# A recurrent attention loop that streams a quarter of its weights: other blocks streamed, other blocks held in PSUM, and a fixed slot for every load

## The chip, the cores and the metric

The kernel runs on one core of a Trainium2 chip. The metric is the time of one execution on the device in microseconds (us). The kernel before takes 2891.25 us, the median of 8 runs (2883.82 to 2897.93). The engines are named as the profile names them: PE (TensorE) multiplies, PEld is its weight load, DVE (VectorE) and ACT (ScalarE) do elementwise work, POOL (GpSimd) copies and issues some DMAs, SP (SyncE) issues most DMAs. Every engine works through its own queue in program order; semaphores make it wait for another engine or a DMA.

## The reference

Two independent results are laid side by side in the output: `a` from a recurrent attention, `b` from a long convolution (a state-space layer).

```python
def _A_ref(x, mem0, Wq, Wk, Wv, Wo, seg_len):        # x 1*2048*1024, 32 heads of 128, seg_len 32
    mem = mem0                                        # 8 rows of 1024
    for s in range(n_seg):                            # 64 segments
        h = concat([mem, x[segment s]], axis=1)       # 40 rows
        q, k, v = h @ Wq, h @ Wk, h @ Wv              # each 1024 -> 32*128
        p = softmax(mask(q @ k.T * scale))            # 40*40 a head
        o = (p @ v) @ Wo                              # 32*128 -> 1024
        mem = o[:, :8]                                # the next segment needs it
        outs.append(o[:, 8:])
```

So segment s+1 can't begin its projections before segment s has multiplied by the last block of `Wo`. Each of the four weights is 1024 x 4096 in bf16, 8 MB; together they are larger than the SBUF that the loop leaves free.

## The kernel before

**Order of the whole.** Part B (the convolution, `part_b`) runs first, and beside it the kernel projects those rows of `x` that need no recurrence (8 of each 32), stores them in DRAM (`PKd`), and copies the weight blocks that will be streamed into DRAM tiles of their own (`WD`, `streamed_copies`). Then comes part A's loop of 64 steps (L289 to L479), one step a segment, with only the 32 rows that need the recurrence in `hT`. A last stage multiplies the rows set aside (`OLd`) by `Wo`.

**Weight blocks.** The weights are cut into 64 blocks of 128 x 2048 in bf16 (512 KB). A block of k, q or v is named (matrix, half t, kc): eight blocks kc = 0..7 make one accumulation of 128 x 512 in `quads` (L293). Below, `k04` stands for ("k", 0, 4). A block of `Wo` is ("o", u), here `o5`; 16 of them are used in `oproj` (L393). In a step PE uses the blocks in this order: k0 (8), q0 (8), k1 (8), q1 (8), v0 (8), v1 (8), o (16). Transposes (`tr`), scores, and the products with the probabilities (`pv`) stand between. A k, q or v block is four matmuls of 128x512, an o block eight of 128x256.

**Three homes of a block.** 46 blocks stay in SBUF through the loop (`RESIDENT`, in the profile `W_k`, `W_q`, `W_v`, `W_o`). 16 blocks are loaded from DRAM in every step; the list is `STREAM` and `STREAM_O`. Two blocks, `KEPT`, stay in PSUM (two banks each) and are copied to SBUF by DVE when they are wanted: `fetch` (L261) makes two copies of 128x512 words by `words` (L251, in the trace L252). Streamed and fetched blocks both lie in the pool `wst`, which has four places of 512 KB, here called slots.

**Who sets the order.** The order of part A is written out by hand (`manual_schedule`). `unit` (L224) is called where PE's matmuls of a block are written; for a streamed block it takes the next slot and issues the load on SP (L230). SP runs ahead of PE as far as slots are free: a load is issued when the block that held its slot before has been used by PE, and the loads leave SP in the order in which the blocks are used. Before the change the pool is one ring of four: the 18 streamed and fetched blocks of a step take the slots in turn, in the order of their `unit` and `fetch` calls, so a fetched block also takes its turn in the ring. `fetch(("q", 0, 0))` stands behind the k0 accumulation (L407), `fetch(("o", 8))` behind the first half of the output projection (L461). DVE makes each copy where it stands in its own queue: q00's just behind the copy of the new memory rows into `hT` (L476, end of the step before), o8's just behind the probabilities of the second half (L459).

**The end of a step.** After o15, DVE copies the result (L470), PE transposes the memory rows (L475), DVE copies them to `hT` (L476), and k00 of the next step begins. POOL issues the loads of the next step's `xt` and `pk` and the writes of `OLd` and of the output (L273, L278, L477, L479).

The functions that the diff touches:

Of the kernel before, what the change touches and what calls it, by code (L numbers as in the profile page):

```python
# [10 lines left out]
BF16 = mybir.dt.bfloat16  # L11
F32 = mybir.dt.float32
# [8 lines left out]
HALF_PI = float(np.pi / 2.0)  # L21


STREAM = {("k", 0): (0, 4), ("q", 0): (0, 4), ("k", 1): (0, 4), ("q", 1): (0, 4), ("v", 0): (0, 4), ("v", 1): (0, 4)}
STREAM_O = (0, 3, 5, 8, 11, 13)

KEPT = {("q", 0, 0): 2, ("o", 8): 2}


def weight_blocks(Wq, Wk, Wv, Wo):  # L30
# [13 lines left out]


def streamed_keys():
    return [key for key in [(m, t, kc) for (m, t), kcs in STREAM.items() for kc in kcs] + [("o", u) for u in STREAM_O] if KEPT.get(key) != 2]


def streamed_copies(ctx, tc, src):  # L50
    nc = tc.nc
    dram = ctx.enter_context(tc.tile_pool(name="a_wd", bufs=1, space=bass.MemoryType.DRAM))
    out, copies = {}, []
    for key in streamed_keys():
        part = KEPT.get(key, 0)
        t_ = dram.tile([128, 2048 - 1024 * part], BF16, name="WD_%s" % "_".join(str(i) for i in key))
        copies.append(lambda t_=t_, key=key, part=part: nc.sync.dma_start(
            out=t_[:].rearrange("e (h d) -> e h d", d=1024) if key[0] == "o" else t_[:], in_=src(key)[:, part:] if key[0] == "o" else src(key)))
        out[key] = t_
    return out, copies  # L60

# [99 lines left out]

RESIDENT = [(m, t, kc) for t in range(2) for m in "kq" for kc in range(8)] + [("v", t, kc) for t in range(2) for kc in range(8)] + [("o", u) for u in range(16)]
RESIDENT = [key for key in RESIDENT if key not in streamed_keys() and key not in KEPT]


# [13 lines left out]
def part_a(ctx, tc, x, mem0, src, WD, HE, seg_len, out_a, ahead, W_res, rest):  # L179
    nc = tc.nc  # L180
# [14 lines left out]

    ctx.enter_context(tc.manual_schedule())
    ctx_w = rest.ctx
    wst = ctx_w.enter_context(tc.tile_pool(name="a_wst", bufs=4, side="right"))
    wres = ctx_w.enter_context(tc.tile_pool(name="a_wres", bufs=1, side="right"))
    for key in rest:  # L200
        load_resident(tc, wres, src, key, W_res)
# [19 lines left out]
    nc.gpsimd.affine_select(out=BDL[:], in_=BDL[:], compare_op=ALU.is_ge, fill=0.0, base=0, pattern=[[-8, 4], [-32, 4]], channel_multiplier=1)  # L221
    nc.gpsimd.affine_select(out=BDL[:], in_=BDL[:], compare_op=ALU.is_ge, fill=0.0, base=7, pattern=[[8, 4], [32, 4]], channel_multiplier=-1)

    def unit(key):  # L224
        if key in W_res:
            return W_res[key]
        if key in kept:
            return ahead_of.pop(key)
        t_ = wst.tile([128, 2048], BF16, name="wst", tag="w")
        nc.sync.dma_start(out=t_[:], in_=WD[key][:])  # L230
        return t_

# [15 lines left out]
    ps_k = ctx_l.enter_context(tc.tile_pool(name="a_keep", bufs=1, space=PSUM))  # L248
    kept, ahead_of = {}, {}

    def words(out, in_):  # L251
        nc.vector.tensor_scalar(out=out.bitcast(I32), in0=in_.bitcast(I32), scalar1=0, scalar2=None, op0=ALU.bitwise_or)  # L252

    for key, n_ in KEPT.items():
        t_ = wst.tile([128, 2048], BF16, name="wst", tag="w")
        nc.sync.dma_start(out=t_[:].rearrange("e (h d) -> e h d", h=2) if key[0] == "o" else t_[:], in_=src(key))
        kept[key] = [ps_k.tile([128, 512], F32, name="keep", tag="keep%d" % (len(kept) * 2 + n)) for n in range(n_)]
        for n in range(n_):
            words(kept[key][n][:], t_[:, 1024 * n:1024 * n + 1024])

    def fetch(key):  # L261

        t_ = wst.tile([128, 2048], BF16, name="wst", tag="w")
        for n in range(2):
            if n < KEPT[key]:
                words(t_[:, 1024 * n:1024 * n + 1024], kept[key][n][:])
            else:
                nc.sync.dma_start(out=t_[:, 1024:2048], in_=WD[key][:])
        ahead_of[key] = t_

    def load_pk(j):
        pk = pers.tile([128, 768], BF16, name="pk", tag="pk")
        nc.gpsimd.dma_start(out=pk[:], in_=PKd[j])  # L273
        return pk

    def load_xt(j):
        xt = work.tile([128, KC, XM], BF16, name="xt", tag="F")
        nc.gpsimd.dma_start(out=xt[:].rearrange("p k r -> p (k r)"), in_=XTd[j])  # L278
        return xt

    def put_xt(xt):
        nc.gpsimd.tensor_copy(out=hT[:, :, 0:XM], in_=xt[:])
# [3 lines left out]

    put_xt(load_xt(0))
    pk = load_pk(0)
    for s in range(NS):  # L289
        vl = pk[:, 512:768].rearrange("p (t e) -> p t e", t=2)  # L290
        kl, ql = ([pk[:, 256 * t + o:256 * t + o + 128].rearrange("p (a g k) -> p a g k", a=4, g=4) for t in range(2)] for o in (0, 128))

        def quads(m, t, kcs, a=None):  # L293
            if a is None:

                a = (ps_sc if (m, t) == ("q", 0) else ps_acc).tile([128, 512], F32, name="acc", tag="sc" if (m, t) == ("q", 0) else "acc")
            for kc in kcs:
                w = unit((m, t, kc))
                for g in range(4):
                    nc.tensor.matmul(a[32 * g:32 * g + 32, :], lhsT=hT[:, kc, :], rhs=w[:, 512 * g:512 * g + 512],  # L300
                                     start=(kc == 0), stop=(kc == KC - 1), tile_position=(0, 32 * g), skip_group_check=True)
            return a

        def evac(a, tag):
            q = work.tile([128, 512], BF16, name="ev", tag=tag)
            nc.scalar.copy(out=q[:], in_=a[:])  # L306
            return q
# [70 lines left out]
        def pv_x(t, V, pb, lbs):  # L378

            p = (ps_pv, ps_sc)[t].tile([128, 4, 128], F32, name="pv", tag=("pv", "sc")[t])  # L380
            pv(p[:], t, V, pb, lbs)
            return p
# [10 lines left out]
        def oproj(po, us, oT):  # L393
            for u in us:
                w = unit(("o", u))
                for hh in range(2):
                    h = 2 * u + hh
                    for qt in range(4):
                        nc.tensor.matmul(po[32 * qt:32 * qt + 32, :], lhsT=oT[:, h % 4, (h % 16) // 4, :],  # L399
                                         rhs=w[:, 1024 * hh + 256 * qt:1024 * hh + 256 * qt + 256],  # L400
                                         start=False, stop=(h == 31), tile_position=(0, 32 * qt), skip_group_check=True)
# [2 lines left out]


        a = quads("k", 0, range(KC))
        fetch(("q", 0, 0))  # L407
        k0 = evac(a, "A")
        KT0 = new_kt(0)
        a = quads("q", 0, range(KC))  # L410
# [47 lines left out]
        spread_l(lb1[:], S1[1][:, 0, :], 0, 16, SL)  # L458
        L1 = left_blocks(S1)  # L459
        oproj(pp[:, 1, :], range(0, 8), o0)  # L460
        fetch(("o", 8))  # L461
        pv1 = pv_x(1, V1, pk[:, 0:512].rearrange("p (a b) -> p a b", a=4), [lb1[:].rearrange("p a k -> p (a k)")])
        o1 = evac_o(pv1, "B")
        pv_l(pl_, 1, V1, L1)
# [7 lines left out]
        if s + 1 < NS:  # L472
            pt_o = ps_pv.tile([128, 2, 4, SL], BF16, name="tro", tag="pv")
            for j in range(2):
                nc.tensor.transpose(out=pt_o[:, j, :, :].rearrange("p a b -> p (a b)"), in_=osb[:, 128 * j:128 * j + 128], identity=ident[:])  # L475
            nc.vector.tensor_copy(out=hT[:, :, XM:SL].rearrange("p (q j) r -> p j q r", j=2), in_=pt_o[:, :, :, XM:SL])  # L476
        nc.gpsimd.dma_start(out=OLd[s], in_=ob[:, 1, :])  # L477

        nc.gpsimd.dma_start(out=out_a[s * SL:s * SL + SL, :].rearrange("r (q d) -> q r d", q=4), in_=osb)  # L479
# [3 lines left out]
    with tc.tile_pool(name="a_eo", bufs=1) as eo, tc.tile_pool(name="a_ew", bufs=16) as ew, \  # L483
# [3 lines left out]
        for u in range(16):  # L487
            if u in (0, 2, 4, 6):
# [3 lines left out]
                for n in range(2):  # L492
                    (nc.vector.tensor_copy if n == 0 else nc.scalar.copy)(
                        out=ol[b][:, 16 * n:16 * n + 16, :, :], in_=raw[:, :, 16 * n:16 * n + 16, :].rearrange("p s h k -> p h s k"))
            w = ew.tile([128, 2048], BF16, name="we", tag="we")
# [3 lines left out]
        for u in range(16):  # L499
            for hh in range(2):  # L500
                h = 2 * u + hh
# [594 lines left out]
def kernel(  # L1096
# [25 lines left out]
    src = weight_blocks(A_Wq.rearrange("d h e -> d (h e)"), A_Wk.rearrange("d h e -> d (h e)"),  # L1122
                        A_Wv.rearrange("d h e -> d (h e)"), A_Wo.rearrange("h e d -> (h e) d"))
    WD, copies = streamed_copies(ctx, tc, src)
    ahead = Ahead(ctx, tc, A_x[0], src, seg_len)
    ctx_w = ctx.enter_context(ExitStack())
# [12 lines left out]
    with ExitStack() as ctx_a:  # L1139
        part_a(ctx_a, tc, A_x[0], A_mem0[0], src, WD, A_Wo.shape[0] * A_Wo.shape[1], seg_len, out_a, ahead, W_res, rest)  # L1140
# [35 lines left out]
```

## Time and profile before

| what | value |
|---|---|
| median of 8 runs | 2891.25 us (2883.82 to 2897.93) |
| the profiled execution's own time | 2889.88 us |
| its span in the profile | 2888.2 us |
| mean granted TensorE clock | 0.917 of full |
| PE, DVE, ACT, POOL busy over the span | 72%, 52%, 34%, 18% |
| one step of the loop, mean of steps 5 to 60, from k00 to k00 | 27.77 us |
| streamed loads | 1024 of 512 KB, 16 a step |

The profile's page gives, by part: busy time of each engine, the span in 40 slices, the DMA queues, the chain of work that ended last, the costliest groups of instructions, and the DMA issues. In a group's line the name left of the arrow is written and those to the right are read: `acc<-wst,hT` is a matmul with a streamed or fetched block, `acc<-W_k,hT` one with a block that stays. `[0.85 <-DMA wst<-WD_k]` at the end of a timeline line is the engine's idle time before it and what ended it. The loop lies in slices 13 to 39 of 40.

### The profile page before, as it was taken

How to read it: one execution, taken by the hardware profiler on the slowest of the kernel's cores; microseconds unless marked ns; L12 is line 12 of the kernel's file. 1: busy time of each engine (PE TensorE's matmuls, PEld its weight loads, DVE VectorE, ACT ScalarE, POOL GpSimd, SP SyncE). 2: the span in 40 equal slices, each digit the busy share in tenths (PEclk: the TensorE clock that was granted, in tenths of full speed). 3: DMA queues.
4: the chain of work that ended last, by engine and by line, in shares of the span. 5: the costliest groups of instructions: out<-in, count | busy, mean ns of one | idle time of the engine just before them, and what ended most of it. 6: DMA issues, size and time to landing. Idle time of an engine off the chain costs nothing.

```text
span 2888.2 us, 76070 instructions
## 1 busy us (share of the span) xinstructions
PE 2077.2 (72%) x32791; PEld 1126.1 (39%) x32838; DVE 1515.5 (52%) x2882; ACT 970.9 (34%) x1394; POOL 516.1 (18%) x801
## 2 busy tenths in 40 slices
PE   1478777846797477777777777777777777777747
PEld 0246444532342144444444344444444444443423
DVE  7577676766984144544544445454454444544430
ACT  4767787741121122222222222222222222222210
POOL 2254434541001111111111111111111111111100
PEclk8699898978898699999999999999999999999978
DMA  4546654525336899999998998999999899998991
GB/s 112 150 147 168 177 158 123 149 86 159 104 117 227 313 323 326 325 325 315 315 328 312 315 324 310 322 314 321 308 326 320 309 323 312 326 316 304 319 308 43
DMA packets 354722, 734.94 MB, mean 254 GB/s; under 512 B 111606, under 2 KB 179190, under 8 KB 352336
## 3 DMA queue, kind: packets, MB, share of 16 engines
q1 hardware_dynamic: 316770, 655.39, 67.4%
q0 software_dynamic: 21840, 52.65, 5.6%
q10 hardware_dynamic: 15774, 22.03, 2.3%
q8 instruction: 257, 4.21, 0.6%
q14 instruction: 81, 0.66, 0.1%
HBM read 675.04 MB, written 67.37 MB: 257 GB/s over the span
## 4 chain that ended last, share of the span: by engine, by line
DMA 40%; PE 23%; issue 18%; ACT 7%; DVE 7%; POOL 4%; SPq 0%; ACTq 0%; POOLq 0%; DVEq 0%
DMA wst<-WD_k 14%; PE acc L300 12%; DMA wst<-WD_o 12%; DMA wst<-WD_v 6%; DMA wst<-WD_q 4%; PE pp L399 3%; ACT ev L306 2%; PE pe L505 2%; DMA olr<-OLd 1%; ACT sn L888 1%; ACT oT L386 1%; PE pro L128 1%; POOL us L772 1%; POOL us L773 1%; PE ups L767 1%
## 5 line engine op out<-in xcount | busy, mean ns | idle before, releaser
L300 PEld LDWEIGHTS <-hT 128*32 128x32 bf16 x12288 | 328.5, 98 | 540.9 <-issue 249.3
L300 PE MATMUL acc<-wst,hT 128*32 128x512 bf16 x3072 | 317.6, 399 | 242.9 <-DMA wst<-WD_k 100.6
L306 ACT CAST ev<-acc 128x512 bf16<-128x512 f32 x384 | 225.1, 586 | 482.7 <-PE acc L300 482.1
L399 PEld LDWEIGHTS <-oT 128*32 128x32 bf16 x8192 | 218.8, 100 | 251.7 <-issue 171.4
L399 PE MATMUL pp<-wst,oT 128*32 128x256 bf16 x3072 | 162.8, 287 | 173.0 <-DMA wst<-WD_o 136.6
L312 DVE COPY KT<-tr 128x512 bf16<-128x512 bf16 x128 | 54.3, 424 | 358.9 <-PE tr L311 358.9
L300 PE MATMUL acc<-W_k,hT 128*32 128x512 bf16 x3072 | 230.9, 406 | 0.0
L300 PE MATMUL acc<-W_q,hT 128*32 128x512 bf16 x3072 | 221.1, 390 | 0.0
L399 PE MATMUL pp<-W_o,oT 128*32 128x256 bf16 x5120 | 221.0, 284 | 0.0
L300 PE MATMUL acc<-W_v,hT 128*32 128x512 bf16 x3072 | 211.4, 379 | 0.0
L338 DVE TENSOR_REDUCE mx<-sc 128x8 f32<-128x320 f32 x128 | 62.2, 486 | 236.4 <-PE sc L331 236.4
L252 DVE TENSOR_SCALAR wst<-keep 128x512 int32<-128x512 int32 x256 | 164.2, 683 | 5.9 <-DMA wst<-WD_k 0.9
L386 ACT CAST oT<-pv 128x512 bf16<-128x512 f32 x128 | 75.3, 588 | 245.2 <-PE pv L372 239.1
L470 DVE CAST ob<-pp 128x256 bf16<-128x256 f32 x64 | 27.2, 425 | 239.5 <-issue 236.3
L312 ACT COPY QT<-tr 128x512 bf16<-128x512 bf16 x128 | 75.0, 586 | 213.5 <-PE tr L311 204.4
L1062 PE MATMUL yp<-Bt,mi 128*128 128x512 bf16 x379 | 116.1, 412 | 32.9 <-DVE Bt L1016 15.0
L980 PE MATMUL hps<-KT,MF 128*128 128x512 bf16 x374 | 100.6, 414 | 50.0 <-DVE x L991 26.4
L319 POOL COPY KT<-pk 128x128 bf16<-128x128 bf16 x128 | 38.2, 299 | 528.8 <-PE sc L331 519.3
L278 POOL DMA_DIRECT2D xt<-XTd x64 | 36.2, 565 | 503.5 <-PE pp L372 245.0
L128 PE MATMUL pro<-xTl,wsl 128*128 128x512 bf16 x492 | 115.4, 384 | 8.8 <-DVE ua L769 4.6
L864 DVE SCALAR_TENSOR_TENSOR nr<-kM,ptt 128x656 f32<-128x656 f32 x128 | 106.0, 828 | 20.7 <-ACT kM L863 17.4
L340 ACT ACTIVATE sc<-sc 128x320 f32<-128x320 f32 x128 | 54.0, 422 | 186.7 <-DVE sc L339 165.2
(266 smaller groups left out, 3838.5 us busy)
## 6 DMA issues: line engine op xcount, KB each, us to landing
wst<-WD_o SPq DMA_DIRECT2D x320, 512.0 KB
wst<-WD_k SPq DMA_DIRECT2D x256, 512.0 KB, 5.1
wst<-WD_v SPq DMA_DIRECT2D x256, 512.0 KB, 5.3
wst<-WD_q SPq DMA_DIRECT2D x192, 512.0 KB
Ud<-ux POOLq DMA_DIRECT2D x16, 1024.0 KB, 5.0
uq<-Ud SPq DMA_DIRECT2D x32, 512.0 KB, 4.9
pk<-PKd POOLq DMA_DIRECT2D x64, 192.0 KB, 5.1
wsl<-in_A_Wk_dram SPq DMA_DIRECT2D x16, 512.0 KB
```

Of the source, the lines that this page charges most:

```text
L128: nc.tensor.matmul(a[:], lhsT=w[:, kc, 128 * j:128 * j + 128], rhs=xTl[:, kc, :, :].rearrange("p s k -> p (s k)"), start=(kc == 0), stop=( ...
L252: nc.vector.tensor_scalar(out=out.bitcast(I32), in0=in_.bitcast(I32), scalar1=0, scalar2=None, op0=ALU.bitwise_or)
L300: nc.tensor.matmul(a[32 * g:32 * g + 32, :], lhsT=hT[:, kc, :], rhs=w[:, 512 * g:512 * g + 512], start=(kc == 0), stop=(kc == KC - 1), til ...
L306: nc.scalar.copy(out=q[:], in_=a[:])
L312: eng(out=dst, in_=p[:, i, :, :, :])
L338: nc.vector.tensor_reduce(out=mx[:], in_=sc, axis=AX.X, op=ALU.max)
L386: nc.scalar.copy(out=o[:], in_=p[:].rearrange("p a (g q) -> p a g q", g=4))
L399: nc.tensor.matmul(po[32 * qt:32 * qt + 32, :], lhsT=oT[:, h % 4, (h % 16) // 4, :], rhs=w[:, 1024 * hh + 256 * qt:1024 * hh + 256 * qt + ...
L505: nc.tensor.matmul(pe[b][n][:], lhsT=ol[b][:, hi, :, :].rearrange("p s k -> p (s k)"), rhs=wos[u][:, 1024 * hh + 512 * n:1024 * hh + 512 * ...
L864: v.scalar_tensor_tensor(out=nrs[e // 4][:, e % 4].rearrange("p f t j -> p f (t j)"), in0=kM[:], scalar=MAGIC, in1=ptv, op0=ALU.subtract, ...
L980: pe.matmul(ps[:], lhsT=MF[:, 4 * rr + mc, cs, 128 * kc:128 * kc + 128], rhs=rhs, start=(i == 0 and mc == 0), stop=(i == 1 and mc == 3))
L1062: pe.matmul(yp[:], lhsT=m_[:, cs, kc, :], rhs=Bt[:, kc, half, j, c_, :], start=(n == 0), stop=(n == 15))
```

## The change

The number of streamed blocks (16), of kept blocks (2), of slots (4) and the computation stay the same. What is different:

- which blocks are streamed: of k0 and q0 before 0, 4 and 4 (with q00 kept), after k00, k06 and q03 (with k04 and q05 kept); of `Wo` before 0, 3, 5, 11, 13 (with o8 kept), after 0, 4, 8, 11, 14;
- the slots: each load takes slot number (count of loads) mod 4, so in every step k00, k14, v04, o4 take slot 0; k06, q10, v10, o8 slot 1; q03, q14, v14, o11 slot 2; k10, v00, o0, o14 slot 3;
- a kept block takes the slot of the block named beside it in `KEPT`: k04 that of o14, between o14's use and k10's load; q05 that of k06, between k06's use and q10's load;
- `fetch(("k", 0, 4))` stands at the end of a step, behind the copy into `hT`; `fetch(("q", 0, 5))` stands where q00's stood in the code, behind k0; there is no fetch in the output projection any more.

```diff
-STREAM = {("k", 0): (0, 4), ("q", 0): (0, 4), ("k", 1): (0, 4), ("q", 1): (0, 4), ("v", 0): (0, 4), ("v", 1): (0, 4)}
-STREAM_O = (0, 3, 5, 8, 11, 13)
-
-KEPT = {("q", 0, 0): 2, ("o", 8): 2}
+
+STREAM = {("k", 0): (0, 6), ("q", 0): (3,), ("k", 1): (0, 4), ("q", 1): (0, 4), ("v", 0): (0, 4), ("v", 1): (0, 4)}
+STREAM_O = (0, 4, 8, 11, 14)
+
+KEPT = {("k", 0, 4): ("o", 14), ("q", 0, 5): ("k", 0, 6)}
+SLOTS = 4
...
-    wst = ctx_w.enter_context(tc.tile_pool(name="a_wst", bufs=4, side="right"))
+    wst = ctx_w.enter_context(tc.tile_pool(name="a_wst", bufs=1, side="right"))
...
+    place, loads = {}, [0]
+
     def unit(key):
         if key in W_res:
             return W_res[key]
         if key in kept:
             return ahead_of.pop(key)
-        t_ = wst.tile([128, 2048], BF16, name="wst", tag="w")
+        place[key] = loads[0] % SLOTS
+        loads[0] += 1
+        t_ = wst.tile([128, 2048], BF16, name="wst", tag="w%d" % place[key])
         nc.sync.dma_start(out=t_[:], in_=WD[key][:])
         return t_
...
     def fetch(key):
 
-        t_ = wst.tile([128, 2048], BF16, name="wst", tag="w")
+        t_ = wst.tile([128, 2048], BF16, name="wst", tag="w%d" % place.get(KEPT[key], SLOTS - 1))
         for n in range(2):
-            if n < KEPT[key]:
-                words(t_[:, 1024 * n:1024 * n + 1024], kept[key][n][:])
-            else:
-                nc.sync.dma_start(out=t_[:, 1024:2048], in_=WD[key][:])
+            words(t_[:, 1024 * n:1024 * n + 1024], kept[key][n][:])
         ahead_of[key] = t_
...
     put_xt(load_xt(0))
     pk = load_pk(0)
+    fetch(("k", 0, 4))
     for s in range(NS):
...
         a = quads("k", 0, range(KC))
-        fetch(("q", 0, 0))
+        fetch(("q", 0, 5))
         k0 = evac(a, "A")
...
         oproj(pp[:, 1, :], range(0, 8), o0)
-        fetch(("o", 8))
...
             nc.vector.tensor_copy(out=hT[:, :, XM:SL].rearrange("p (q j) r -> p j q r", j=2), in_=pt_o[:, :, :, XM:SL])
+            fetch(("k", 0, 4))
```

The rest of the diff drops the case of a block kept in part, and gives the loads that fill PSUM before the loop slots 0 and 1.

More of the change, by code (lines that the diff above doesn't have):

```diff
@@ L46, in streamed_keys @@
 def streamed_keys():
-    return [key for key in [(m, t, kc) for (m, t), kcs in STREAM.items() for kc in kcs] + [("o", u) for u in STREAM_O] if KEPT.get(key) != 2]
+    return [key for key in [(m, t, kc) for (m, t), kcs in STREAM.items() for kc in kcs] + [("o", u) for u in STREAM_O]]
 def streamed_copies(ctx, tc, src):
@@ L54, in streamed_copies @@
     for key in streamed_keys():
[L55 to L58, printed above, removed]
+        t_ = dram.tile([128, 2048], BF16, name="WD_%s" % "_".join(str(i) for i in key))
+        copies.append(lambda t_=t_, key=key: nc.sync.dma_start(
+            out=t_[:].rearrange("e (h d) -> e h d", h=2) if key[0] == "o" else t_[:], in_=src(key)))
         out[key] = t_
@@ L252, in words @@
         nc.vector.tensor_scalar(out=out.bitcast(I32), in0=in_.bitcast(I32), scalar1=0, scalar2=None, op0=ALU.bitwise_or)
-    for key, n_ in KEPT.items():
-        t_ = wst.tile([128, 2048], BF16, name="wst", tag="w")
+    for i, key in enumerate(KEPT):
+        t_ = wst.tile([128, 2048], BF16, name="wst", tag="w%d" % i)
         nc.sync.dma_start(out=t_[:].rearrange("e (h d) -> e h d", h=2) if key[0] == "o" else t_[:], in_=src(key))
-        kept[key] = [ps_k.tile([128, 512], F32, name="keep", tag="keep%d" % (len(kept) * 2 + n)) for n in range(n_)]
-        for n in range(n_):
+        kept[key] = [ps_k.tile([128, 512], F32, name="keep", tag="keep%d" % (2 * i + n)) for n in range(2)]
+        for n in range(2):
             words(kept[key][n][:], t_[:, 1024 * n:1024 * n + 1024])
     def fetch(key):
-        t_ = wst.tile([128, 2048], BF16, name="wst", tag="w")
+        t_ = wst.tile([128, 2048], BF16, name="wst", tag="w%d" % place.get(KEPT[key], SLOTS - 1))
         for n in range(2):
-            if n < KEPT[key]:
-                words(t_[:, 1024 * n:1024 * n + 1024], kept[key][n][:])
-            else:
-                nc.sync.dma_start(out=t_[:, 1024:2048], in_=WD[key][:])
+            words(t_[:, 1024 * n:1024 * n + 1024], kept[key][n][:])
         ahead_of[key] = t_
```

## The prediction

> **What bounds the kernel now.** I read the page's slices and chain first, to see which stage and which resource end the time:
>
> ```profile
> span 2888.2 us, 76070 instructions
> ...
> DMA  4546654525336899999998998999999899998991
> GB/s 112 150 147 168 177 158 123 149 86 159 104 117 227 313 323 326 325 325 315 315 328 312 315 324 310 322 314 321 308 326 320 309 323 312 326 316 304 319 308 43
> ...
> DMA 40%; PE 23%; issue 18%; ACT 7%; DVE 7%; POOL 4%; SPq 0%; ACTq 0%; POOLq 0%; DVEq 0%
> DMA wst<-WD_k 14%; PE acc L300 12%; DMA wst<-WD_o 12%; DMA wst<-WD_v 6%; DMA wst<-WD_q 4%; PE pp L399 3%; ACT ev L306 2%; PE pe L505 2%; DMA olr<-OLd 1%; ACT sn L888 1%; ACT oT L386 1%; PE pro L128 1%; POOL us L772 1%; POOL us L773 1%; PE ups L767 1%
> ```
>
> The loop is slices 13 to 39; there the largest links of the chain are the streamed loads. About 320 GB/s looks like a full DMA, but single microseconds of the loop reach 422 GB/s, so the loads are not at a ceiling of bytes. I then asked for the waits in 1200 to 2800 us, and for the tile wst:
>
> ```profile
> PE pp L399 <- DMA wst<-WD_o: 120.6, 163, 2.1
> PE acc L300 <- DMA wst<-WD_k: 90.8, 101, 2.5
> PE acc L300 <- DMA wst<-WD_v: 24.1, 31, 1.7
> PE acc L300 <- DMA wst<-WD_q: 14.4, 34, 1.2
> ```
>
> ```profile
> L252 DVE TENSOR_SCALAR wst<-keep x226: 677/680/693, 1219.8 to 2777.5; 128x512 int32<-128x512 int32 x113
> ...
> DMA to landing us min/median/max: 3.9/5.2/6.9
> ```
>
> PE loses 250 us in 57 steps, 4.4 us a step, to loads, and a load needs 5.2 us from issue to landing. The timeline of one step shows the slots:
>
> ```profile
> 2004.04 1.29 DVE L252 TENSOR_SCALAR wst<-keep 128x512 int32<-128x512 int32 x2
> 2004.06 0.40 PE L300 MATMUL acc<-wst,hT 128*32 128x512 bf16 x4 [0.33 <-PE tro L475]
> ...
> 2004.50 1.49 SPq L230 DMA_DIRECT2D wst<-WD_k  x2
> ...
> 2009.21 0.40 PE L300 MATMUL acc<-wst,hT 128*32 128x512 bf16 x4 [0.85 <-DMA wst<-WD_k]
> ...
> 2020.84 0.40 PE L300 MATMUL acc<-wst,hT 128*32 128x512 bf16 x4
> ...
> 2024.60 1.27 DVE L252 TENSOR_SCALAR wst<-keep 128x512 int32<-128x512 int32 x2
> ...
> 2026.21 0.40 PE L399 MATMUL pp<-wst,oT 128*32 128x256 bf16 x8 [0.52 <-ACT oT L386]
> ...
> 2031.37 1.29 DVE L252 TENSOR_SCALAR wst<-keep 128x512 int32<-128x512 int32 x2
> 2031.39 0.40 PE L300 MATMUL acc<-wst,hT 128*32 128x512 bf16 x4 [0.33 <-PE tro L475]
> ```
>
> k00 is used at 2004.06, and SP issues k10 into its slot at 2004.50; PE uses k10 at 2009.21 after a stall. v14 is used at 2020.84; its slot goes to o8, which DVE brings only at 2024.60 and PE uses at 2026.21: for 5.4 us no load could use that slot.
>
> Over steps 5 to 60 I paired each load's issue with its landing and its first matmul in the trace. Means, time 0 being k00's first matmul:
>
> | load | issue | takes | used | waits in slot |
> |---|---|---|---|---|
> | k04 | -3.78 | 5.36 | 1.68 | 0.11 |
> | k10 | 0.45 | 5.04 | 5.75 | 0.26 |
> | k14 | 2.16 | 5.16 | 7.47 | 0.14 |
> | v00 | 6.20 | 5.59 | 12.33 | 0.55 |
> | o0 | 12.78 | 5.43 | 18.53 | 0.33 |
> | o13 | 20.15 | 5.13 | 25.57 | 0.29 |
>
> With two loads still in flight at the issue one takes 5.06 us, with three 5.57: the loop is bound by slot time, not bytes. The budget of a step: 4 slots x 27.77 = 111.1 us = 16 loads x 5.27 (84.4) + landing to end of use (13.1) + slots taken by the kept blocks + 1.3 (rest). The kept part: q00 from o11's end (24.82) to its own (27.77 + 3.15) is 6.1 us, o8 from 17.78 to 23.94 is 6.2, together 12.3.
>
> **The change part by part.**
>
> *Copies by DVE.* Still two fetches of 2 x 0.68 us a step. o8's leaves the output projection, where 8 waits on it cost PE 5.3 us in all: 0.1 us a step. k04's stands where q00's copy stands now: it starts with the step (2004.04 against 2004.06) and takes 1.29, so k04 can start at 1.31. Without that wait PE would be there at 0.87 (the shortest k00 to k04 in the trace): 0.44 us of new wait. Today k04 comes at 1.68, so this is no loss against today. q05's copy waits for k06's last matmul: 1.31 + 2 x 0.215 + 0.41 = 2.15, and the copy ends at 3.5. PE would be at q05 at about 3.2, so PE waits some 0.3. Behind that copy DVE next has the copy to KT (L312), at 2008.40 (4.3) in the step shown: covered; without that cover it would delay the scores by as much. The added fetch before the loop is at most 1.3 us, once.
>
> *Kept slot time.* k04: o14's end to k04's end. o13's end to k00 is 1.76; o14 is one block (0.2) later, so 1.55 + 1.31 + 0.41 = 3.3. q05: from 2.15 to 3.55 + 0.41, 1.8. Together 5.1 instead of 12.3: 7.2 us of slot time a step set free.
>
> *The fixed slots.* That saving isn't even. Slots 0 and 2 hold no kept block, slot 1 holds q05, slot 3 holds k04 and then must bring k10. SP can issue k10 only after k04's use: 1.31 + 0.41 + 0.05 = 1.77 instead of 0.45. k14 and all later loads stand behind it in SP's queue; k14 goes out at 2.10 (one issue is 0.32), which is no later than today's 2.16, and q10 at about 4.0, q14 at 4.3 (today 4.20). Follow slot 3 with today's durations: k10 1.77 + 5.04, used at 6.85, end 7.26; v00 issued 7.3, takes 5.59, used 12.95, end 13.35; o0 13.4 + 5.43, used 18.9, end 19.3; o14 19.35 + 5.2 (the median), used 24.6, end 25.0; to the next k00 another 1.55. A step of 26.6 us, if PE is never late for these four. Today it is late: v00 and o0 wait 0.55 and 0.33 in their slots, and the least wait is 0.04 to 0.05, so 0.8 us. Sum: 27.4 us.
>
> The same sum for today's ring checks the method. Each slot there passes nine blocks in two steps; one slot has k10, v00, o0, o11, q00, q10, v10, o5, k00: 42.0 (its eight loads) + 8 x 0.46 + 6.1 = 51.8 in two steps, 25.9 a step, the other pair of slots 26.4, against 27.77 found. So waits add 1.4 to 1.9 there, and 0.8 in mine is the low end; I take 0.8 because k10 and o14 are to be waited for by PE itself, as k14 and k04 are now (0.14, 0.11).
>
> *Bounds of what no row shows.* The latency of k10 when issued beside the writes of OLd and the output, into an emptier queue: from 4.7 (loads whose predecessor had 1.5 to 2.5 us to go) to 5.4 (k04's today, beside the load of pk). I take 5.04, k10's own row. If all four loads took 5.57 (three in flight), slot 3 needs +1.0 us; waits in the slots as large as the ring's (1.9) add 1.1; no waits at all, -0.8.
>
> *Other queues.* No POOL or ACT instruction moves; the 16 loads keep their size and order of issue. The rest of the program is unchanged apart from which blocks are loaded once.
>
> *Sum.* 27.4 instead of 27.77 is -0.35 us, rounded to -0.3 for the k06 to q05 wait that may leak into slot 3; x 63 = -19 us. The profiled execution took 2889.88 (span 2888.2), so 2871; it stands 1.4 below the median, which gives 2872.
>
> The Trainium skill, page "DMA: Bandwidth & Descriptors", section on the anatomy of one DMA, gives about 2.0 us plus bytes over 436 GB/s for a software-issued transfer; as an estimate 512 KB would take 3.2 us. The trace's minimum is 3.9 and its median 5.2, so I don't use it. By it a slot would turn over in 3.7 us, neither kernel would wait for slots, and the change would bring nothing.
>
> **The rivals.**
>
> *A, all freed slot time comes through.* (111.1 - 7.2) / 4 = 25.97 us a step, -1.8 x 63 = -113: 2778. If the fuller queue takes half of the way from 5.27 to 5.57 a load, +0.6 us: about 2815. For it: the budget closes to 1%. Against: slot 3's own round of 26.6 us before any wait, and PE waits in order, so one slow slot holds the other three.
>
> *B, slower: slot 3's round becomes the bound at a fuller queue's latency.* Place: k10, v00, o0 and o14, seen first at the first matmul of k1, 1.1 us later than today (6.85 against 5.75). My four durations have a mean of 5.32; the step is 27.77 again when the mean is 5.41, and that is where it decides. With three loads in flight at all four issues (5.57) the step is 26.6 + 0.8 + 1.0 = 28.4: +0.65 x 63 = +41, 2931. For it: loads that spread evenly keep the queue full, and today's loads in the full stretch take 5.4 to 6.1. Against: k10 is issued with one load or two in flight, and o8's stop in the ring is gone, where o5 to o8 holds 1.66 us at the least, in which o8 can land.
>
> *C, no change.* Slot 3's round replaces the ring's at the same length (26.6 + 1.1): 2880 to 2900.
>
> **How the numbers follow.** This forecast 0.35 (2855 to 2882), A 0.13, B 0.32, C 0.20. What a measurement of this kernel can tell from no change is about 0.3%, 8.7 us, so 2882.6 to 2899.9. Faster: 0.13 + 0.33 = 0.46; the same 0.21; slower 0.33. The range reaches from A with the fuller queue (2815) to most of B (2925, a mean of 5.54); beyond lie A's full gain and the rest of B, about 0.15 together. My own forecast's range alone is 2855 to 2882.
>
> **What would show it.** Right: k10's load issued at 1.7 to 1.9 us after k00, its first matmul near 6.9 with most of PE's waits on WD_k there; DMA waits before o blocks much shorter than 120.6 us; two L252 pairs at about 0 and 2.2 us in the step; the deepest queue (three in flight) from v00 to o14. Wrong: a step of 26 us (the four slots share the gain), a mean over 5.41 in slot 3, q05's copy held longer than 0.3 us, or a wait at o4, o8 or o11 as long as those at o3 and o5 now.

## The result, and the profile after

The changed kernel takes 2867.42 us (median of 12 runs, 2857.55 to 2880.11) against 2892.62 (33 runs): a ratio of 0.9917 over all runs, 95% interval 0.9900 to 0.9934 (of the two medians 0.9913). Measured once more beside the last experiments the ratio was 0.9942 (0.9918 to 0.9966). The forecast was 2872, faster. The size is right; the reason given for it is not, as the experiments show.

A part of the gain may be the clock's. The granted TensorE clock is 0.928 in the mean of the changed kernel's runs, and 0.919 in before's runs beside the experiments; among runs of one and the same kernel, 0.01 more clock goes with about 7 us less (129 runs), so some 6 or 7 of the 24 us are left open by this, as an estimate. In the second measurement (0.922 against 0.920) it is 2 of 16 us, and experiment 9, at 0.918 against 0.920, is faster than before by about as much: the rest of the gain isn't the clock's.

The profiled execution took 2868.38 us (span 2866.7), 21.5 less than before's 2889.88. From the first k00 to the last the loop is 1726.4 us, before it was 1747.6: the loop accounts for 21.2 of them. First the page, by the lines that were shown of before:

```profile
span 2866.7 us, 75691 instructions
...
DMA  4545654425345889999999999989898999899981
GB/s 112 149 153 163 172 166 128 141 85 162 101 131 198 323 310 318 330 319 324 332 319 320 325 333 330 330 317 330 312 334 303 324 331 315 305 324 328 317 304 37
...
DMA 36%; PE 21%; issue 19%; DVE 12%; ACT 7%; POOL 4%; SPq 1%; ACTq 0%; DVEq 0%; POOLq 0%
DMA wst<-WD_k 11%; PE acc L303 11%; DMA wst<-WD_q 8%; DMA wst<-WD_o 8%; DMA wst<-WD_v 3%; ACT oT L389 2%; PE pe L508 2%; PE pp L402 2%; DMA olr<-OLd 1%; ACT sn L891 1%; POOL us L775 1%; DMA PVd<-vst 1%; POOL us L776 1%; PE pro L129 1%; ACT ev L309 1%
```

The loads' share of the chain falls from 40% to 36%, and within it from k, o and v to q; DVE's rises from 7% to 12%. Then the waits of the changed kernel in 1200 to 2770 us (57 steps, as before; the columns are us in total, times, longest):

```profile
PE acc L303 <- DMA wst<-WD_k: 92.5, 104, 2.6
...
PE pp L402 <- DMA wst<-WD_o: 58.4, 98, 1.9
...
PE acc L303 <- DMA wst<-WD_q: 41.0, 61, 2.5
```

PE's waits for o blocks halve (120.6 to 58.4), those for q blocks triple (14.4 to 41.0). In the same stretch, the waits of SP's queue:

```profile
SPq L235 <- PE acc L303: 395.1, 569, 2.1
SPq L235 <- DVE wst L257: 301.2, 113, 4.8
```

Before, in 1200 to 2760 us, the second line read:

```profile
SPq L230 <- DVE wst L252: 46.6, 45, 1.8
```

The last line of the tile wst, after the change:

```profile
DMA to landing us min/median/max: 4.6/6.0/8.1
```

Neither is in the forecast's sum. SP now waits 301.2 us for the copied blocks instead of 46.6, and loads take longer: the median of those that this view pairs (two of the 16 of a step, k00 and v04) goes from 5.2 to 6.0 us, the mean over all of them from 5.32 to 5.52. A step in the timeline of the changed kernel shows the places:

```profile
2042.62 1.28 DVE L257 TENSOR_SCALAR wst<-keep 128x512 int32<-128x512 int32 x2
...
2042.80 0.40 PE L303 MATMUL acc<-wst,hT 128*32 128x512 bf16 x4 [0.33 <-PE tro L477]
...
2043.66 0.68 PE L303 MATMUL acc<-wst,hT 128*32 128x512 bf16 x4
...
2044.37 1.61 SPq L235 DMA_DIRECT2D wst<-WD_k  x2
2044.46 0.40 PE L303 MATMUL acc<-wst,hT 128*32 128x512 bf16 x4
...
2044.90 1.29 DVE L257 TENSOR_SCALAR wst<-keep 128x512 int32<-128x512 int32 x2 [1.01 <-PE acc L303]
...
2046.67 0.79 SPq L235 DMA_DIRECT2D wst<-WD_q  x2
...
2048.95 0.40 PE L303 MATMUL acc<-wst,hT 128*32 128x512 bf16 x4 [1.55 <-DMA wst<-WD_k]
```

k00 begins at 2042.80; k04 follows at 2043.66, PE using its first half before DVE has copied the second; at 2044.37 SP sends the loads of k10 and k14 one behind the other, when k04 is used, although k14's slot has been free since k00; at 2046.67 q10 and q14 leave the same way behind q05. k10 is waited for at 2048.95.

**The budget of slot time.** The forecast's budget, 4 slots x step = loads + waits in the slot + use + slots held for a kept block + issue delay (from the end of the slot's last use to the issue), was counted for each kernel from the trace, as means over steps 6 to 60, in us a step (one step fewer than in the forecast, so 27.80 and not 27.77). For the loads of before the forecast had 84.4 us and a rest of 1.3; here they are 85.0, and the rest is 0.7, the issue delay. It is an account and closes by its nature; what it tells is where freed time goes:

| kernel | step | 4 x step | loads (mean of one) | waits | use | kept | issue delay |
|---|---|---|---|---|---|---|---|
| before | 27.80 | 111.2 | 85.0 (5.32) | 6.6 | 6.6 | 12.3 | 0.7 |
| after | 27.32 | 109.3 | 88.3 (5.52) | 6.3 | 6.5 | 5.0 | 3.1 |
| ring | 28.49 | 114.0 | 82.9 (5.18) | 6.7 | 6.7 | 17.1 | 0.7 |
| old blocks | 29.44 | 117.8 | 88.3 (5.52) | 7.6 | 6.7 | 7.9 | 7.2 |
| swap of k1 | 27.35 | 109.4 | 89.9 (5.62) | 6.2 | 6.6 | 5.1 | 1.6 |
| double swap | 27.13 | 108.5 | 90.1 (5.63) | 6.2 | 6.5 | 5.1 | 0.7 |
| old o blocks | 27.33 | 109.3 | 86.8 (5.43) | 7.5 | 6.7 | 5.2 | 3.1 |
| k07 kept | 27.94 | 111.7 | 87.9 (5.49) | 6.2 | 6.6 | 6.4 | 4.6 |
| no writes | 26.71 | 106.8 | 86.5 (5.41) | 5.7 | 6.5 | 4.9 | 3.2 |
| half loads | 23.79 | 95.2 | 53.1 (3.32) | 28.7 | 6.4 | 4.2 | 2.8 |
| before, slots redealt | 27.45 | 109.8 | 87.9 (5.49) | 6.7 | 6.5 | 7.9 | 0.7 |
| double swap, old o blocks | 26.88 | 107.5 | 87.6 (5.47) | 7.4 | 6.8 | 5.2 | 0.7 |
| double swap again | 26.95 | 107.8 | 89.5 (5.60) | 6.0 | 6.5 | 5.1 | 0.7 |
| after again | 27.41 | 109.6 | 88.6 (5.54) | 6.2 | 6.6 | 5.1 | 3.2 |

Each row is one execution: the two of the changed kernel differ by 0.1 us a step, the two of the double swap by 0.2. Of the 7.3 us that the kept blocks give up, 2.4 go into issue delay and 3.3 into longer loads; with 0.3 less of waits and use 1.9 us are left, 0.48 a step by these steps (21.2 / 63 = 0.34 over the whole loop).

### The profile page after: what moved, and what is told of

It reads as the page before. It is cut to its first block, busy times and chain, and to the rows that moved or that the text cites. A ratio compares the mean times of both kernels' runs of the same rounds, so it can differ in the third digit from the quotient of the medians.

```text
span 2866.7 us, 75691 instructions
## 1 busy us (share of the span) xinstructions
PE 2079.2 (73%) x32791; PEld 1109.4 (39%) x32838; DVE 1516.6 (53%) x2882; ACT 970.1 (34%) x1394; POOL 517.7 (18%) x801
## 4 chain that ended last, share of the span: by engine, by line
DMA 36%; PE 21%; issue 19%; DVE 12%; ACT 7%; POOL 4%; SPq 1%; ACTq 0%; DVEq 0%; POOLq 0%
DMA wst<-WD_k 11%; PE acc L303 11%; DMA wst<-WD_q 8%; DMA wst<-WD_o 8%; DMA wst<-WD_v 3%; ACT oT L389 2%; PE pe L508 2%; PE pp L402 2%; DMA olr<-OLd 1%; ACT sn L891 1%; POOL us L775 1%; DMA PVd<-vst 1%; POOL us L776 1%; PE pro L129 1%; ACT ev L309 1%
## 5 line engine op out<-in xcount | busy, mean ns | idle before, releaser
L303 PE MATMUL acc<-wst,hT 128*32 128x512 bf16 x3328 | 362.6, 397 | 264.9 <-DMA wst<-WD_k 143.8
L303 PEld LDWEIGHTS <-hT 128*32 128x32 bf16 x12288 | 319.8, 97 | 589.4 <-issue 294.4
L402 PEld LDWEIGHTS <-oT 128*32 128x32 bf16 x8192 | 210.4, 96 | 165.6 <-issue 86.8
L303 PE MATMUL acc<-W_q,hT 128*32 128x512 bf16 x3072 | 236.9, 386 | 0.0
L402 PE MATMUL pp<-W_o,oT 128*32 128x256 bf16 x5632 | 211.9, 273 | 0.6 <-issue 0.6
L402 PE MATMUL pp<-wst,oT 128*32 128x256 bf16 x2560 | 128.3, 276 | 97.9 <-DMA wst<-WD_o 64.3
```

## The experiments

**1. The new blocks in the old ring.**

```diff
-wst = tile_pool(name="a_wst", bufs=1); tag="w%d" % place[key]
+wst = tile_pool(name="a_wst", bufs=4); tag="w"
```

> The blocks, their places and the two fetches of the changed kernel, but the slots of the kernel before: one ring of four. If the streamed blocks' even spread brings the gain (rival), this is as fast as the changed kernel, 2867 us. If slot time sets the step (my theory), it is slower than both: k04's fetch then takes the slot of o4 (free at 20.6 us of a step of 27.3, needed until 1.6 of the next, 8.4 us), q05's that of o14 (6.2 us), together 14.6 us of slot time against 5.0 in the changed kernel, so (14.6 - 5.0) / 4 = 2.4 us a step or more, since q03 can be loaded only after k04's use: 3000 to 3050 us.

Measured: 2945.05 us, ratio 1.0187 (1.0145 to 1.0229). The even spread of the blocks doesn't bring the gain; with the ring it is lost and more. The loss is smaller than expected: the kept blocks hold 17.1 us, but with fewer loads in flight one takes 5.18 us instead of 5.52. A load's time gives way.

**2. The old blocks in fixed slots.**

```diff
-STREAM = {("k", 0): (0, 6), ("q", 0): (3,), ...}; STREAM_O = (0, 4, 8, 11, 14)
-KEPT = {("k", 0, 4): ("o", 14), ("q", 0, 5): ("k", 0, 6)}
+STREAM = {("k", 0): (0, 4), ("q", 0): (4,), ...}; STREAM_O = (0, 3, 5, 11, 13)
+KEPT = {("q", 0, 0): ("o", 13), ("o", 8): ("o", 5)}
```

> The fixed slots of the changed kernel with the streamed and kept blocks of the kernel before: q00 takes o13's slot, fetched at the end of the step; o8 takes o5's slot. Kept slot time is 4.9 (q00: 1.6 + 3.15 + 0.2) + 2.2 (o8) = 7.1 us against 12.3 before. If the slots share what is freed (budget theory, rival A of the prediction): (111.1 - 5.2) / 4 = 26.5 us a step, 2810 us. If the round of the slot that must bring k10 sets the step (my theory): k10 can be issued only after q00's use at 3.2 us instead of 1.65, so the step is about 1.5 us longer than the changed kernel's 27.33, near 28.9: 2960 to 2975 us, slower than both.

Measured: 2999.25 us, 1.0376 (1.0341 to 1.0411). SP's queue, from the timeline of this kernel, one line a run of issues:

```profile
2006.66 0.32 SPq L235 DMA_DIRECT2D wst<-WD_q  x1
2014.36 0.79 SPq L235 DMA_DIRECT2D wst<-WD_k  x2
2015.21 0.90 SPq L235 DMA_DIRECT2D wst<-WD_q  x2
```

For 7.4 us SP issues nothing, then four loads within 1.8 us: k10 waits for q00's slot, and k14 and q10 stand behind it for 4.0 and 2.2 us although their slots are free: most of the 7.2 us of issue delay. It is slower still than the theory of the slot's round had it (2960 to 2975 us), and the budget without issue delay (2810) is far off. Kept time alone fell by 4.4 us and promised a gain; so what a kept block costs is also what it holds up in SP's queue.

**3. k10 and k14 change slots.**

```diff
-place[key] = loads[0] % SLOTS
+n = loads[0] % 16
+if n == 0:
+    step_slots[:] = [place.get(("o", u), i) for i, u in enumerate((4, 8, 11, 14))]
+place[key] = step_slots[SLOT_OF[n]]   # SLOT_OF = (0, 1, 2, 0, 3, 1, 2, 0, 3, 1, 2, 0, 3, 1, 2, 0)
```

> The changed kernel, but k10 takes the slot that k00 leaves at 0.42 us and k14 the one that k04 leaves at 1.62 (in the changed kernel it is the other way round, and k14's load waits on SP behind k10's); everything after follows in the same order. Slot time in total is unchanged. Budget theory: no change against the changed kernel, 2867 us. My theory (the round of k04, k10, v00, o0, o14 is the longest): k04's stop now falls on each of two slots in every second step, k10 is issued 1.2 us earlier and lands near 5.3 instead of 6.19; a step of 26.3 to 26.8, 0.5 to 1.0 us less, 2805 to 2835 us.

Measured: 2873.28 us, 0.9925 (0.9886 to 0.9964): the same as the changed kernel. k10 is issued at 0.47 us instead of 1.65 and used at 5.76 instead of 6.28, but the step stays at 27.35. The waits of this kernel (1200 to 2760 us) show where the half microsecond goes:

```profile
PE acc L307 <- DMA wst<-WD_q: 75.6, 99, 2.5
...
PE pp L406 <- DMA wst<-WD_o: 53.2, 96, 2.4
PE acc L307 <- DMA wst<-WD_k: 53.0, 68, 2.2
```

The wait for k blocks falls from 92.5 to 53.0 and that for q blocks rises from 41.0 to 75.6: q10, whose slot comes free behind q05's copy, is late instead. The theory that the round of slot 3 sets the step fell here. In the budget 1.5 us of issue delay turned into 1.6 us of longer loads.

**4. q10 and q14 change slots too.** `SLOT_OF = (0, 1, 2, 0, 3, 2, 1, 0, 3, 2, 1, 0, 3, 2, 1, 0)`

> As the run before, and q10 takes the slot that q03 leaves at 4.23 us, q14 the one that q05 leaves at 4.76. My theory: q10 waits for its landing in 43% of the steps of the changed kernel, so up to 0.2 us a step more than the swap of k10 and k14 alone, 2795 to 2830 us. Budget theory: 2867 us.

Measured: 2850.73 us, 0.9864 (0.9835 to 0.9893). Now every load takes the slot that has been free longest, and the issue delay falls from 3.1 to 0.7 us a step. SP's line against DVE's copies shrinks from 301.2 us (the same view and nearly the same stretch, 1200 to 2760):

```profile
SPq L239 <- DVE wst L261: 19.7, 49, 0.4
```

That line isn't the delay itself: the kernel of experiment 9, whose issue delay is 0.7 us as well, has 152.1 us on it (1200 to 2770). What counts is how long a free slot goes unused.

**5. The old o blocks in the changed kernel.** `STREAM_O = (0, 3, 5, 11, 13)`, k04 in o13's slot.

> The changed kernel with the streamed o blocks of the kernel before (0, 3, 5, 11, 13; k04 takes the slot of o13); o8 stays in SBUF, o4 and o14 too. The swap of k10 and k14 has shown that the round of slot 3 does not set the step, so that theory is given up. New theory: between k00 and k10 the changed kernel is 0.53 us slower than the one before, and its whole gain, 0.93 us a step, lies between o0 and o8, where two loads (o0, o4) are now wanted instead of three (o0, o3, o5) before PE has to wait for DVE anyway. Then this run loses most of it: o5's load takes v10's slot at 16.7 us, lands near 21.7, and o8 can begin only 1.7 to 2.1 us after it, near 23.8 instead of 23.06: 27.33 + 0.75 = 28.1 us a step, 2900 to 2918 us. Rival (freed slot time alone, wherever the blocks lie): k04 holds its slot 0.2 us longer, 2867 to 2872 us.

Measured: 2859.46 us, 0.9886 (0.9847 to 0.9925): not slower than the changed kernel. So the theory formed after the third run fell as well. PE waits for o3 and o5 as it did before the change (o5 is used 0.04 us after landing), but k00 and k06 then go out earlier (-7.3 and -5.7 us instead of -6.7 and -3.8), q03, issued at -2.7 instead of -3.0, takes 5.3 us instead of 6.6, k10 is used at 5.56, and the step is 27.33 again. Where in the step PE waits is not where the time is decided.

**6. k07 kept instead of k04.** `KEPT = {("k", 0, 7): ("o", 14), ...}`

> The changed kernel with k07 instead of k04 kept in PSUM, in the same slot: PE waits no more for the copy, but the slot comes free after k07's use at about 3.05 us instead of 1.62, so k10 is issued 1.4 us later. Slot 3's round as the bound: +1.4 us a step, 2955 us. Slot time shared by all: +0.35 us, 2890 us. Waits that replace each other (new theory): k10 is used at 7.7 instead of 6.28, but q10, which lands at 9.6 and is now waited for, takes 0.4 us of it back: +0.9 to 1.0 us, 2920 to 2932 us.

Measured: 2918.13 us, 1.0085 (1.0054 to 1.0117), between the second and the third expectation, 51 us over the changed kernel; 0.62 us a step in the profile. In the budget the kept time grows by 1.4 and the issue delay by 1.5 (k14, behind k10, 3.0 instead of 1.6), loads fall by 0.4: 2.4 / 4 = 0.6. k10's own load, issued later into an emptier queue, takes 3.8 us instead of 4.5.

**7. Without the writes at the end of a step.**

```diff
+nc.gpsimd.dma_start(out=OLd[:], in_=PKd[:, :, 0:256])   # before the loop
...
-nc.gpsimd.dma_start(out=OLd[s], in_=ob[:, 1, :])
-nc.gpsimd.dma_start(out=out_a[...], in_=osb)
+if s + 1 == NS:
+    nc.gpsimd.dma_start(out=out_a[...], in_=osb)
```

> The changed kernel without the two DMA writes that POOL issues at the end of each step (the output rows and OLd, 64 KB each); one copy fills OLd before the loop, and the output rows of all steps but the last are not written. k06 and q03, in flight then, take 6.06 and 6.59 us where a load takes 5.5 in the mean, and PE waits for them. If the writes are the cause: both land about 0.5 us earlier, q05's copy and the load of q10 behind it too, 0.3 to 0.5 us a step less, 2835 to 2850 us. If the cause is the queue of loads itself (three in flight at their issue) or the load of pk: no more than 0.1 us, 2861 to 2869 us.

Measured: 2860.41 us, 0.9879 (0.9845 to 0.9913). The total misleads here: the copy that fills OLd before the loop moves the first k00 from 1006.2 to 1028.1 us. The step falls by 0.6 us, from 27.32 to 26.71, more than either expectation had. The place was wrong: k06 and q03 hardly gain (they land at 2.11 and 3.46 instead of 2.24 and 3.64); k10, k14 and q10 gain, from 4.54, 5.66 and 4.83 us a load to 3.78, 4.95 and 4.17, while v00, v04 and v10 behind them take 0.2 to 0.3 us longer. Why k06 and q03 take over 6 us is therefore not the writes; whether it is the loads ahead of them or the load of pk stays open.

**8. Half of each load.**

```diff
-nc.sync.dma_start(out=t_[:], in_=WD[key][:])
+nc.sync.dma_start(out=t_[:, 0:1024], in_=WD[key][:, 0:1024])
...
-rhs=w[:, 512 * g:512 * g + 512]
+rhs=w[:, 512 * (g % 2):512 * (g % 2) + 512]
```

> The changed kernel, where each streamed load brings only the first half of its block (256 KB) and every matmul of q, k, v and o blocks reads that half twice; the slots, their order and the number of PE instructions stay. The result is not the reference's product. It parts a load's fixed time from that of its bytes. If the time of a load is mostly fixed (a wait of about 4.5 us whatever the size), loads still take 4.3 to 4.8 us and the step is 25 to 26 us, 2720 to 2780. If it is mostly the queue of bytes, loads take 3.3 to 3.9 us and the step falls to what PE, DVE and the copies need, 23 to 24 us, 2590 to 2655.

Measured: 2640.27 us, 0.9125 (0.9084 to 0.9165). From this kernel's tile wst in 1200 to 2760 us:

```profile
DMA to landing us min/median/max: 2.5/3.1/5.1
```

A mean load takes 3.32 us instead of 5.52: two fifths of a load's time vanish with half the bytes of all of them. If time goes with bytes in a straight line, 2 x 2.2 = 4.4 of the 5.52 us belong to the bytes and the rest to a fixed wait. That is an estimate: fewer loads are in flight too (53.1 / 23.79 = 2.2 instead of 88.3 / 27.32 = 3.2), and this run doesn't part the two. In the step of 23.79 us PE still waits for k10 and k14 (49.6 us in 55 steps), so the loads at their full size cost at least 3.5 us a step.

**9. The kernel before, only its slots dealt out anew.** Its blocks and its two fetches stay where they were; o8 takes the slot of o5 instead of v14's, and each load the slot that has been free longest.

```diff
-t_ = wst.tile(..., tag="w")                        # a ring of four
+place[key] = place.get(AFTER[key], loads[0])       # o11 after v14, o13 after o0, k00 after o3, ...
+t_ = wst.tile(..., tag="w%d" % place[key])
```

> The kernel before with its own streamed and kept blocks and its own places of the two fetches, in the code; only the slots are dealt out differently: o8 takes the slot of o5 and not that of v14, q00 that of o11 as before, and every load takes the slot that has been free longest, so no load stands in SP's queue behind one that waits. Slot time of the kept blocks: q00 6.1, o8 21.7 to 23.9 = 2.2, together 8.3 instead of 12.3 us. Budget with longer loads: of the 4.0 us freed, two thirds to three quarters go into longer loads, as between before and the changed kernel (3.3 of 4.9) and between the changed kernel and the double swap (1.8 of 2.4); 1.0 to 1.3 us are left, divided by four slots 0.25 to 0.33 us a step, x 63: 2870 to 2877 us. Budget without longer loads: 2829. If the gain of the changed kernel came from which blocks it streams and keeps (rival): no change, 2888 to 2896.

Measured: 2873.51 us, 0.9951 (0.9925 to 0.9978); beside it the changed kernel 2875.62. The total is as expected, and with none of the changed kernel's blocks the gain can't be told from its own. The budget: kept 4.4 less, loads 2.9 more (two thirds), no issue delay added. The changed kernel frees more (7.3) and wastes 2.4 of it in SP's queue.

**10 to 12. Double swap with the old o blocks, double swap again, changed kernel again.**

> The double swap with the streamed o blocks of the kernel before (0, 3, 5, 11, 13). If the even spread of the o blocks is worth nothing, as the earlier run with them showed for the changed kernel, this equals the double swap, 2843 to 2858 us. If the spread is worth something once no load waits in SP's queue, it is 10 to 40 us slower, 2860 to 2890.

> The double swap once more, beside the changed kernel on one chip: 16 to 17 us faster than it, ratio to before 0.985 to 0.988, if the slot time that SP's queue wastes in the changed kernel (2.4 us a step) is what makes the difference; equal to it if the first measurement was chance.

> The changed kernel itself, as a yardstick for the three others: 2860 to 2875 us, ratio to before 0.990 to 0.9935.

Measured on the same chip: 2847.39 us, 0.9858 (0.9823 to 0.9893); 2850.55 us, 0.9857 (0.9824 to 0.9890); 2875.62 us, 0.9942 (0.9918 to 0.9966). The double swap beats both kernels in both measurements, 17 to 25 us faster than the changed one; which o blocks are streamed makes no difference there either.

## Why the prediction was right, and where it was not

- *What bounds the kernel.* Right as to slot time: slots alone, without any change of blocks, move the time in both directions (experiments 1 and 9). "Not bytes" went too far. Over 1200 to 2500 us the 16 DMA engines are busy 0.92 of the time before the change (318 GB/s), 0.91 after it (323) and 0.93 in the double swap (325), but 0.61 with half loads (195); the single microsecond of 422 GB/s has a DMA share of 1.05 in its own row, so it says little about a ceiling. Slots and bytes are tied: a freed slot puts one more load into a nearly full queue. How far above that rate the loop could get wasn't tried.
- *Kept slot time.* 5.1 us forecast, 5.0 found; 12.3 before, as forecast.
- *Copies by DVE.* q05's copy follows k06's last matmul, as described, but from 2.94 to 4.22 us in the mean and not from 2.15 to 3.5. k04's costs less: PE starts with the first half, at 0.95 us instead of 1.31, so k10 is issued at 1.65 instead of 1.77. The sum let k06 follow k04 without a wait, at 1.74 us, and q05 at 3.55; k06 was used at 2.43, q03 at 3.81 and q05 at 4.26, because the loads of k06 and q03 took 6.1 and 6.6 us. The eight waits of 5.3 us that the forecast gives to o8's copy are three before q00 (3.6 us) and five before o8 (1.6 us); nothing hangs on it.
- *Slot 3's round.* This is the step that failed, and that the number came out all the same is luck. The sum is met, four loads of 21.26 us forecast and 21.28 found, but one by one they are 4.51, 5.78, 5.08 and 5.91 instead of 5.04, 5.59, 5.43 and 5.2: errors of up to 0.7 us that cancel. Waits beyond the least one were 0.8 in the forecast and are 1.0 (1.15 in all); the round is the step, 27.32, against 27.4. But every slot's round equals the step once its waits are counted in, so the sum showed that this slot could be the bound, not that it was. Experiment 3 brought k10 forward by half a microsecond and changed nothing; experiment 6 held the slot 1.4 us longer, and the step grew by 0.6.
- *SP's queue.* That k14 stands behind k10, and later loads behind both, was seen (under the fixed slots) and priced at nothing because they were to leave hardly later than before. k14 does leave at 2.03 us (2.16 before); q10 and q14 leave at 4.80 and 5.17, where the forecast had 4.0 and 4.3. Counted in slot time, k14 behind k10 and q14 behind q10 cost 2.4 us a step (1.6 and 0.9 of delay), and undoing it (experiment 4) is worth 17 to 25 us. This is the term that was missed.
- *Rival A* was right in its mechanism: the freed slot time is shared by all slots. Its price was wrong: it left out the issue delay (2.4 us), and let the 16 loads grow by at most 2.4 us where they grew by 3.3.
- *Rival B* did not come: the mean of slot 3's four loads is 5.32 us, below its 5.41.
- The rise of a load's time with the queue, taken in the forecast only as a bound (5.06 with two in flight, 5.57 with three), is what keeps all these gains small. Of what "kept" and "issue delay" give up together, two thirds came back as longer loads in the change (3.3 of 4.9) and with the slots redealt (2.9 of 4.4), over three quarters in the double swap (1.8 of 2.3), all of it in the swap of k1 (1.6 of 1.4). These shares are rough: in the second measurement of the double swap beside the changed kernel it was 1.0 of 2.5, with the old o blocks 0.7 of 2.5.
- *The signs.* k10's issue (1.65 us), the short waits for o blocks (58.4 against 120.6) and most waits on WD_k (92.5) came. k10's use near 6.9 didn't (6.28), nor the second copy at 2.2 (2.94); and three loads are in flight not only from v00 on but also when k00 and q03 are issued.

The Trainium skill's page "DMA: Bandwidth & Descriptors", in its section on issuing engines, says that transfers started by SP, ACT and POOL all run on the same 16 DMA engines and interleave. Experiment 7 agrees: taking two writes away from POOL's queue made three of SP's loads 0.7 us shorter each.

## What to carry to other kernels

Where a small pool of buffers feeds an engine, add up buffer time, buffers x period = transfer + wait + use + everything else that holds a buffer, and count what stands behind a waiting DMA in its queue as well; give each load the buffer that has been free longest. Expect only a part of the freed time back when transfers share a queue that is nearly full: by the times of the runs (their difference / 63 x 4 slots) a quarter to a third here where kept blocks gave up slots (1.6 of 4.9 us in the change, 1.1 of 4.4 with the slots redealt), and half or more where the issue delay was undone (1.1 of 2.3 and 1.6 of 2.5). Don't take a chain through one buffer for the bound because it adds up to the period: shorten it in a run and see whether the period follows.

## What the runs showed of the hardware

- Two writes of 64 KB a step (1.5% of the 8.76 MB that a step moves) cost 0.6 us of 27.3, more than 2% (one execution of each; two of the changed kernel differ by 0.1). They move rows of 512 bytes, where the loads move rows of 4 KB; whether the rows are the reason wasn't tried.
- The time of a 512 KB load and the number in flight rise together: 5.18 us in the mean with 82.9 / 28.49 = 2.9 loads at once in the ring of experiment 1, 5.63 us with 90.1 / 27.13 = 3.3 in the double swap. The two come from one account (loads at once = 16 x mean time / step), so neither is the cause of the other; what the pair shows is that 14% more loads in flight brought only 5% more loads per us (16 / 28.49 = 0.56, 16 / 27.13 = 0.59).
